# Attention before a routed expert layer: stacking queries and keys with their hash bits into one 71-row contraction, and using the exp tile as the stationary operand for V

## The chip, the cores and the metric

The kernel runs on one core of a Trainium2 chip. The metric is the device time of one execution in microseconds (us). A unit in this text is one pass of the attention's main loop.

## The reference

Attention over four batches of eight heads (768 positions, 64 dimensions). Each query and key gets six hash bits (the signs of a projection), and a query sees only the keys with the same six bits. A query that no key matches gets the mean of V; for its sake both kernels add a tiny multiple of the sums of V. The result feeds a layer of eight experts whose weights come from a Sinkhorn iteration.

```python
q_bits = (np.einsum('bhsd,dk->bhsk', q, proj) > 0)
k_bits = (np.einsum('bhsd,dk->bhsk', k, proj) > 0)
mask   = q_bucket[:, :, :, None] == k_bucket[:, :, None, :]
scores = np.where(mask, scale * (q @ k.T), -1e9)
attn   = softmax(scores) @ v
x      = attn.transpose(0, 2, 1, 3).reshape(B * S, H * D)     # 3072 x 512
P      = sinkhorn(exp(x @ w_gate))                            # 8 rounds
out    = sum(P[:, e:e+1] * (relu(x @ w1[e]) @ w2[e]) for e in range(8))
```

Both kernels write the mask as arithmetic. Bits are coded as plus or minus one half and one side is scaled by a large constant, so that the product of the bits, with a constant row beside them, is zero when all six agree and far below zero when one differs. It is added to the score by the same accumulation on TensorE, and exp then gives zero.

## The kernel before

Work goes by groups: one batch and half of its heads (four), eight groups in all. A unit is a group, a chunk of 256 queries and two key tiles, so there are 72 units. While batches 1, 2 and 3 are in attention, the first expert's matmuls of the batch before are put between the units; the text calls these pieces filler (16 pieces of four 128x384 matmuls, 12 of four 128x512, per batch). The experts' own part follows the attention and takes two thirds of the time.

```python
def scores(n, qc, kp, pairs):              # one unit: both score buffers, two exps
    for hs in pairs:
        st = [sps.tile([P, 2, 2 * QC], F32, tag="s", name="st") for _ in range(len(hs) // 2)]
        for kk in range(2):
            for part in range(3):          # hash bits, then two halves of 32 dimensions
                for i, h in enumerate(hs):
                    lw = d["kb"][sl, ks] if part == 0 else d["k"][sl, part - 1, ks]
                    rw = d["qb"][sl, qs] if part == 0 else d["q"][sl, part - 1, qs]
                    pin(nc.tensor.matmul(st[i // 2][:, i % 2, kk * QC:(kk + 1) * QC], lw, rw,
                                         start=(part == 0), stop=(part == 2), skip_group_check=True))
        for s_ in st:
            pt = wk.tile([P, 2, 2 * QC], F16, tag="p", name="pt", bufs=4)
            pin(nc.scalar.activation(out=pt, in_=s_, func=Act.Exp, scale=scale))
# ... (cut) values(): V slices of 32 columns are stationary and the exp tile moves;
#     a third pass with a tile of ones gives the denominator, which two transposes
#     and a reciprocal on VectorE turn into a factor for the normalising step
for u, (n, qc, kp) in enumerate(units):    # main loop, cut
    nxt = scores(*units[u + 1], four if b else two) if u + 1 < len(units) else None
    values(n, qc, kp, pts)
    pts = nxt
    for _ in range(2):
        next(prep, None)                   # a step of the next group's preparation
    if left > 0:
        got, end = take(fill, left / slots - 200)   # filler
```

The preparation of the next group transposes k and q in blocks of 32x32 on VectorE (L209, 0.95 us for each 128x768), casts them on GpSimd and computes the bits. Four heads lie side by side in four strips of 32 rows, which is how the matmuls read them: no copy is needed.

The softmax here doesn't subtract the row's maximum and nothing guards it: scores larger than these inputs give would overflow.

Of the kernel before, what the change touches and what calls it, by code (L numbers as in the profile page):

```python
# [19 lines left out]
def kernel(  # L20
# [35 lines left out]
    QC = 256  # L56
    NQC = S // QC
    KP = KT // 2
# [9 lines left out]
    pb = consts.tile([P, 2, P], F32)  # L68
# [5 lines left out]
    for a in range(HG):  # L74
        sl = slice(32 * a, 32 * (a + 1))
        for o in (0, 8):
            nc.vector.tensor_copy(pb[sl, :, 32 * a + o:32 * a + o + NB], proj4[sl])
# [4 lines left out]
    nc.vector.tensor_scalar(row_i, row_i, 31, None, op0=Alu.bitwise_and)  # L82
    row_f = consts.tile([P, 1], F32)
    nc.vector.tensor_copy(row_f, row_i)
    coef = consts.tile([P, 1], F32)
    thr = consts.tile([P, 1], F32)
    step = consts.tile([P, 4], F32)
    for i, edge in enumerate((NB - 0.5, NB + 0.5, 7.5, 7.5 + NB)):
        nc.vector.tensor_scalar(step[:, i:i + 1], row_f, edge, None, op0=Alu.is_lt)
    nc.vector.tensor_scalar(thr, step[:, 0:1], 1.0, 1e30, op0=Alu.subtract, op1=Alu.mult)  # L90
    nc.vector.tensor_scalar(coef, step[:, 0:1], 2.0 * BIG - 2.0 * NB * (BIG / 2.0), None, op0=Alu.mult)
    for i, w in ((1, 2.0 * NB * (BIG / 2.0)), (2, BIG), (3, -BIG)):
        nc.vector.scalar_tensor_tensor(coef, step[:, i:i + 1], w, coef, op0=Alu.mult, op1=Alu.add)
    ones = consts.tile([P, P], F32)
    nc.gpsimd.memset(ones, 1.0)
    ones16 = consts.tile([P, R], F16)
    nc.gpsimd.memset(ones16, 1.0)
# [10 lines left out]
    def load_w(e, which, pin=False):  # L108
        if which == 1:
            t = wpool.tile([P, DO, F], F16, tag="w1")  # L110
            src = moe_w1[e].rearrange("(g h c d) f -> g c h d f", g=NGRP, h=HG, c=2)
            for do in range(DO):
                ins = nc.gpsimd.dma_start(out=t[:, do, :], in_=src[do // 2, do % 2])  # L113
                if pin:
                    tc.keep_in_program_order(ins)
            pin = False
        else:
            t = wpool.tile([P, FO, DD], F16, tag="w2")
            ins = nc.gpsimd.dma_start(out=t, in_=moe_w2[e].rearrange("(fo fi) d -> fi fo d", fi=P))
        if pin:  # L120
            tc.keep_in_program_order(ins)
        weights[e, which] = t
# [45 lines left out]
    ld = actx.enter_context(tc.tile_pool(name="ld", bufs=3))  # L168
    lv = actx.enter_context(tc.tile_pool(name="lv", bufs=2))
    wk = actx.enter_context(tc.tile_pool(name="wk", bufs=2))  # L170
    sps = actx.enter_context(tc.tile_pool(name="sps", bufs=2, space=PSUM))
    avs = actx.enter_context(tc.tile_pool(name="avs", bufs=1, space=PSUM))
# [19 lines left out]
    def prepare(n):  # L192

        d = grp[n] = {}
        v16 = wk.tile([P, HG, KT, D], F16, tag="v16")
        vs32 = wk.tile([P, HG, 3, D], F32, tag="vs32", bufs=1)
        vs16 = wk.tile([P, HG, D], F16, tag="vs16")
        for name in ("k", "q"):
            tr = wk.tile([P, 2, S], F32, tag="tr")
            src = nat[name, n]  # L200
            for c in range(2):
                i_ap = src[:, :, 32 * c:32 * (c + 1)]
                o_ap = tr[:, c, :]
                if name == "k":
                    i_ap = i_ap.rearrange("p (m t) d -> p m t d", m=M4)
                    o_ap = o_ap.rearrange("p (t m r) -> p m t r", t=KT, m=M4)
                else:
                    o_ap = o_ap.rearrange("p (m r) -> p m r", r=R)
                pin(nc.vector.transpose(o_ap, i_ap))  # L209
                yield None  # L210
            t16 = wk.tile([P, 2, S], F16, tag=name + "16", name=name + "16")
            for c in range(2):
                nc.gpsimd.tensor_copy(t16[:, c, :], tr[:, c, :])
            bt = wk.tile([P, S], F16, tag=name + "b", name=name + "b")
            for i in range(2):
                sl = slice(i * HT, (i + 1) * HT)
                pr = ops.tile([P, 512], F32, tag="o", name="pr")
                for c in range(2):
                    pin(nc.tensor.matmul(pr[:, 0:HT], pb[:, c, :], tr[:, c, sl], start=(c == 0), stop=(c == 1)))  # L219
                if name == "k":  # L220
                    pin(nc.vector.tensor_scalar(bt[:, sl], pr[:, 0:HT], thr[:, 0:1], coef[:, 0:1],
                                                op0=Alu.is_gt, op1=Alu.mult))
                else:
                    pin(nc.vector.tensor_scalar(bt[:, sl], pr[:, 0:HT], 0.0, 0.5,
                                                op0=Alu.is_gt, op1=Alu.subtract))
                yield 640
            d[name], d[name + "b"] = t16, bt
        for i in range(2):
            nc.gpsimd.tensor_copy(v16[:, 2 * i:2 * i + 2].rearrange("p h t d -> p h (t d)"), nat["v", n, i])
        nc.gpsimd.tensor_tensor(vs32, v16[:, :, 0:3, :], v16[:, :, 3:6, :], op=Alu.add)  # L230
        nc.gpsimd.tensor_tensor(vs32[:, :, 0], vs32[:, :, 0], vs32[:, :, 1], op=Alu.add)
        nc.gpsimd.tensor_tensor(vs16, vs32[:, :, 0], vs32[:, :, 2], op=Alu.add)
        yield None
        vp = ops.tile([P, 512], F32, tag="o", name="vp")
        for c in range(2):
            for h in range(HG):
                pin(nc.tensor.matmul(vp[32 * h:32 * (h + 1), c:c + 1], vs16[:, h, 32 * c:32 * (c + 1)],
                                     ones16[:, 0:1], start=True, stop=True))
        vs = wk.tile([P, 2], F32, tag="vs")
        pin(nc.vector.tensor_scalar(vs, vp[:, 0:2], EPS, None, op0=Alu.mult))  # L240
        d["v"], d["vs"] = v16, vs
        yield 300

    def scores(n, qc, kp, pairs):
        d = grp[n]
        tiles = []
        for hs in pairs:
            st = [sps.tile([P, 2, 2 * QC], F32, tag="s", name="st") for _ in range(len(hs) // 2)]
            for kk in range(2):
                for part in range(3):  # L250
                    for i, h in enumerate(hs):
                        sl = slice(32 * h, 32 * (h + 1))
                        qs = slice(qc * QC, (qc + 1) * QC)
                        ks = slice((2 * kp + kk) * P, (2 * kp + kk + 1) * P)
                        lw = d["kb"][sl, ks] if part == 0 else d["k"][sl, part - 1, ks]
                        rw = d["qb"][sl, qs] if part == 0 else d["q"][sl, part - 1, qs]
                        pin(nc.tensor.matmul(st[i // 2][:, i % 2, kk * QC:(kk + 1) * QC], lw, rw,  # L257
                                             start=(part == 0), stop=(part == 2), skip_group_check=True))
            for s_ in st:
                pt = wk.tile([P, 2, 2 * QC], F16, tag="p", name="pt", bufs=4)  # L260
                pin(nc.scalar.activation(out=pt, in_=s_, func=Act.Exp, scale=scale))  # L261
                tiles.append(pt)
        return tiles

    av = {}

    def values(n, qc, kp, pts):
        d = grp[n]
        if kp == 0:
            av["n"] = avs.tile([P, 2, QC], F32, tag="n", name="num")  # L270
            av["d"] = avs.tile([P, QC], F32, tag="d", name="den")
        num, den = av["n"], av["d"]
        for kk in range(2):
            kt = 2 * kp + kk
            first, last = kt == 0, kt == KT - 1
            for part in range(3):
                for h in range(HG):
                    sl = slice(32 * h, 32 * (h + 1))
                    mv = pts[h // 2][:, h % 2, kk * QC:(kk + 1) * QC]
                    if part < 2:  # L280
                        pin(nc.tensor.matmul(num[sl, part, :], d["v"][:, h, kt, 32 * part:32 * (part + 1)], mv,  # L281
                                             start=first and part == 0, stop=last, skip_group_check=True))
                    else:
                        pin(nc.tensor.matmul(den[sl, :], ones16, mv, start=first, stop=last))  # L284
        if kp == KP - 1:
            b, g = groups[n]
            dt = wk.tile([P, QC], F32, tag="dt")
            pin(nc.vector.transpose(dt, den))
            r8 = wk.tile([P, QC // R], F32, tag="r8")
            pin(nc.vector.tensor_scalar(r8, dt.rearrange("p (a r) -> p a r", r=R)[:, :, 0], S * EPS, None,  # L290
                                        op0=Alu.add))
# [272 lines left out]
```

## Time and profile before

| | before |
|---|---|
| time, median (lowest to highest) | 901.59 us (900.67 to 903.22), 4 runs |
| span of the profiled run | 899.6 us |
| first exp of the attention starts | 27.6 us |
| last exp ends | 284.7 us |
| last gate to the end (experts) | 610.9 us |

The first lines are from the page: busy time of each engine, then the chain of waits that ended last as shares of the span, then groups of instructions by line (busy time, mean of one in ns, then the idle time before them and what ended it).

```profile
PE 830.8 (92%) x7120; PEld 443.1 (49%) x7120; DVE 475.7 (53%) x886; ACT 383.4 (43%) x643; POOL 154.1 (17%) x151
...
PE 63%; DVE 8%; issue 1%; ACT 0%
...
L261 ACT ACTIVATE pt<-st 128x1024 f16<-128x1024 f32 x144 | 139.5, 1021 | 141.4 <-PE st L257 141.1
...
L219 PE MATMUL pr<-tr,pb 128*128 128x384 f32 x128 | 49.8, 528 | 14.9 <-DVE tr L209 9.4
```

ScalarE (ACT) spends 139.5 us in exp and stands idle as long again, 141.4 us, before exps, nearly all of it for the scores (25.6 us of it before the first one). Of the 257 us from the first exp to the last the exps have 54%. The chain of waits could be followed back only to 238 us here, so it says nothing of the first three batches. L219 is the fp32 product that gives the hash bits.

The next view gives busy time by engine in three stretches: the attention of batch 1, the experts from the last gate on, and a piece from the middle of the experts.

```profile
core 0: us, PE busy (x) PEld busy (x) DVE busy (x) ACT busy (x) POOL busy (x), PEclk, DMA share, GB/s
91.00:156.00 65.00, 61.58 (x982) 34.46 (x978) 34.16 (x71) 32.94 (x34) 15.25 (x20) 1.00 0.37 88
288.70:899.60 610.90, 580.02 (x3031) 297.12 (x3028) 329.83 (x572) 241.06 (x494) 80.25 (x58) 0.98 0.18 32
340.00:600.00 260.00, 258.19 (x1361) 132.80 (x1359) 140.03 (x235) 114.34 (x231) 36.04 (x27) 1.00 0.19 28
```

In the middle of the experts TensorE (PE) is busy 258 of 260 us: there is little to win there without taking matmuls away, and the change takes none. In the attention exp is busy 33 of 65 us. The timeline, with the first exp of all and then one unit of batch 1, shows why both cannot be full:

```profile
27.62 1.94 ACT L261 ACTIVATE pt<-st 128x1024 f16<-128x1024 f32 x2 [25.60 <-PE st L257]
...
165.12 0.29 PE L257 MATMUL st<-qb,kb 32*128 32x256 f16 x4
...
166.05 1.94 ACT L261 ACTIVATE pt<-st 128x1024 f16<-128x1024 f32 x2 [3.95 <-PE st L257]
...
168.07 0.29 PE L257 MATMUL st<-qb,kb 32*128 32x256 f16 x4
...
169.00 1.02 ACT L261 ACTIVATE pt<-st 128x1024 f16<-128x1024 f32 x1 [1.00 <-PE st L257]
```

The scores start at 165.12, the two exps run from 166.05 to 167.99, and the next scores start at 168.07. One unit fills both score buffers, so scores and exp take turns: 2.95 us per unit, of which exp is 1.94.

### The profile page before, as it was taken

Reading aid. Unit: us, or ns where it says so; the run is one execution under the profiler, and the core shown is the slowest. Engines: PE = TensorE matmul, PEld = TensorE weight load, DVE = VectorE, ACT = ScalarE, POOL = GpSimd, SP = SyncE. Lnnn points to the kernel's source line nnn. Section 1 sums busy time; section 2 is a strip of 40 time slices with the busy share of each in tenths; the row PEclk is TensorE's granted clock in tenths of the full one; section 3 lists DMA queues with packets and bytes.
Section 4 is the critical chain, followed back from the end, with each engine's and each line's share of the span. In section 5 each row is a group of like instructions: output and inputs, shape, how many; then the busy total and the mean of one; then the engine's idle time right before and its main releaser. Section 6 shows DMA issues by size and latency. Waiting matters only on the chain.

```text
span 899.6 us, 16739 instructions
## 1 busy us (share of the span) xinstructions
PE 830.8 (92%) x7120; PEld 443.1 (49%) x7120; DVE 475.7 (53%) x886; ACT 383.4 (43%) x643; POOL 154.1 (17%) x151
## 2 busy tenths in 40 slices
PE   3788999999899879999999999999999999999992
PEld 1455554555555435555555555555555555555541
DVE  3334564554755765555555555555555555555551
ACT  0466455455465435554333343333333333333330
POOL 3442131221201340014004001400310140000000
PEclk9799999999999889999999999999999999999997
DMA  6941343620000213033003302400330140001222
GB/s 176 190 132 63 102 84 73 152 70 5 1 3 2 33 16 47 1 43 52 1 1 48 47 1 30 65 1 1 48 48 1 20 75 2 1 1 46 78 81 78
DMA packets 37362, 43.07 MB, mean 48 GB/s; under 512 B 15784, under 2 KB 28072, under 8 KB 37288
## 3 DMA queue, kind: packets, MB, share of 16 engines
q0 software_dynamic: 27328, 16.84, 13.1%
q1 hardware_dynamic: 9960, 25.17, 9.3%
q8 instruction: 55, 0.90, 0.4%
q14 instruction: 19, 0.16, 0.1%
HBM read 52.45 MB, written 6.29 MB: 65 GB/s over the span
## 4 chain that ended last, share of the span: by engine, by line
PE 63%; DVE 8%; issue 1%; ACT 0%
PE yp L140 31%; PE a L474 15%; PE d L474 12%; DVE hT L483 3%; PE st L257 1%; PE num L281 1%; PE yp L328 1%; DVE p L413 1%; PE hp L320 1%; PE hp L161 0%; DVE rs L410 0%; DVE xT L298 0%; DVE p L423 0%; DVE xd L440 0%; PE cpt L418 0%
## 5 line engine op out<-in xcount | busy, mean ns | idle before, releaser
L140 PE MATMUL yp<-t,hT 128*128 128x512 f16 x1392 | 375.1, 380 | 0.0
L479 ACT COPY u<-a 128x384 f32<-128x384 f32 x336 | 161.1, 480 | 255.9 <-PE a L474 251.3
L483 DVE CUSTOM_DVE_ANT_0 hT<-d,u 128x384 f16<-128x384 f32 x336 | 179.3, 554 | 144.7 <-PE d L474 88.4
L261 ACT ACTIVATE pt<-st 128x1024 f16<-128x1024 f32 x144 | 139.5, 1021 | 141.4 <-PE st L257 141.1
L140 PEld LDWEIGHTS <-hT 128*128 128x128 f16 x1392 | 136.4, 98 | 116.7 <-issue 0.9
L146 DVE SCALAR_TENSOR_TENSOR acc<-yp,p,acc 128x512 f32<-128x512 f32 x168 | 125.9, 749 | 114.6 <-PE yp L140 112.2
L474 PEld LDWEIGHTS <-t 128*128 128x128 f16 x896 | 87.8, 98 | 78.6 <-issue 11.2
L474 PE MATMUL d<-xd,t 128*128 128x384 f16 x448 | 109.3, 326 | 3.9
L474 PE MATMUL a<-xT,s 128*128 128x384 f16 x448 | 109.5, 326 | 0.0
L474 PEld LDWEIGHTS <-s 128*128 128x128 f16 x672 | 65.9, 98 | 83.4 <-issue 8.1
L509 ACT ACTIVATE hT<-a 128x384 f16<-128x384 f32 x112 | 55.0, 491 | 74.1 <-PE a L474 73.5
L113 POOL DMA_DIRECT2D t<-in_moe_w_dram x32 | 21.4, 675 | 297.1 <-PE d L474 287.8
L257 PE MATMUL st<-q,k 32*128 32x256 f16 x1152 | 63.6, 274 | 0.0
L219 PE MATMUL pr<-tr,pb 128*128 128x384 f32 x128 | 49.8, 528 | 14.9 <-DVE tr L209 9.4
L281 PE MATMUL num<-pt,v 128*32 128x256 f16 x1152 | 53.3, 277 | 9.5 <-DVE xT L298 9.2
L257 PE MATMUL st<-qb,kb 32*128 32x256 f16 x576 | 55.1, 277 | 3.7 <-ACT pt L261 1.7
L474 PE MATMUL d<-xT,t 128*128 128x384 f16 x224 | 55.1, 328 | 0.0
L474 PE MATMUL a<-xT,t 128*128 128x384 f16 x224 | 55.1, 328 | 0.0
L474 PE MATMUL a<-xd,s 128*128 128x384 f16 x224 | 54.8, 326 | 0.0
L284 PE MATMUL den<-pt,ones 128*32 128x256 f16 x576 | 41.1, 275 | 0.0
L219 PEld LDWEIGHTS pr<-tr,pb 128*128 128x128 f32 x128 | 23.4, 197 | 35.5 <-DVE tr L209 15.0
L257 PEld LDWEIGHTS <-k 32*128 32x128 f16 x1152 | 38.9, 95 | 1.9
(73 smaller groups left out, 545.5 us busy)
## 6 DMA issues: line engine op xcount, KB each, us to landing
t<-in_moe_w_dram POOLq DMA_DIRECT2D x8, 1024.0 KB, 9.1
t<-in_moe_w_dram POOLq DMA_DIRECT2D x32, 256.0 KB, 10.4
k<-in_k_dram SPq DMA_DIRECT2D x8, 768.0 KB
q<-in_q_dram SPq DMA_DIRECT2D x8, 768.0 KB
v<-in_v_dram SPq DMA_DIRECT2D x32, 192.0 KB
out_dram<-acc SPq DMA_DIRECT2D x24, 256.0 KB
wg_sb<-in_moe_w_gate_dram POOLq DMA_DIRECT2D x4, 2.0 KB, 8.8
proj<-in_proj_dram SPq DMA_DIRECT2D x2, 3.0 KB
```

The source lines that it names most:

```text
L113: ins = nc.gpsimd.dma_start(out=t[:, do, :], in_=src[do // 2, do % 2])
L140: yield nc.tensor.matmul(yp, hT[:, fo, j * P:(j + 1) * P], w2[:, fo, :], start=(fo == 0), stop=(fo == FO - 1))
L146: nc.vector.scalar_tensor_tensor(out=acc[:, blk, :], in0=yp, scalar=pw[:, blk, e:e + 1], in1=acc[:, blk, :], op0=Alu.mult, op1=Alu.add)
L219: pin(nc.tensor.matmul(pr[:, 0:HT], pb[:, c, :], tr[:, c, sl], start=(c == 0), stop=(c == 1)))
L257: pin(nc.tensor.matmul(st[i // 2][:, i % 2, kk * QC:(kk + 1) * QC], lw, rw, start=(part == 0), stop=(part == 2), skip_group_check=True))
L261: pin(nc.scalar.activation(out=pt, in_=s_, func=Act.Exp, scale=scale))
L281: pin(nc.tensor.matmul(num[sl, part, :], d["v"][:, h, kt, 32 * part:32 * (part + 1)], mv, start=first and part == 0, stop=last, skip_group ...
L284: pin(nc.tensor.matmul(den[sl, :], ones16, mv, start=first, stop=last))
L474: yield nc.tensor.matmul(bk, wq[wn][:, do, f * P:(f + 1) * P], xq[xn][:, do, :], start=first and do == 0, stop=do == 1, skip_group_check=True)
L479: nc.scalar.copy(t, bk)
L483: add(TENSOR_ADD_SAT, out=dst, in0=bk, in1=u, s0=3e38, s1=0.0)
L509: nc.scalar.activation(out=hT[:, f, hi], in_=a, func=Act.Relu)
```

## The change

The intent is to break that chain. A score tile becomes one contraction of 71 rows (64 dimensions, six bits, one constant row), so a unit is one head and one key tile with one score buffer, and the next unit's scores run while exp works. There are 192 units. The exp tile becomes the stationary operand and V, with a column of ones, moves in 65 columns: the denominator comes out in the last column, already one per query, and needs no transposes. The price is that each score matmul reads the 71 rows of a head as one block, so they have to be put under each other. Copies by DMA (called stacking copies below) bring the strips of 32 rows into that place, and the bits go through a scratch tensor in DRAM.

```diff
-            for i in range(2):
-                pr = ops.tile([P, 512], F32, tag="o", name="pr")
-                for c in range(2):
-                    pin(nc.tensor.matmul(pr[:, 0:HT], pb[:, c, :], tr[:, c, sl], start=(c == 0), stop=(c == 1)))
+                nc.gpsimd.tensor_copy(t16[:, c, :], tr[:, c, :])
+                for h in range(HG):
+                    nc.sync.dma_start(out=st[32 * c:32 * (c + 1), h, :], in_=t16[32 * h:32 * (h + 1), c, :])
+                yield None
+            for c in range(2):
+                for j in range(HG):
+                    pin(nc.tensor.matmul(pr[32 * j:32 * (j + 1), 0:QT], pb[:, c].rearrange("p a r -> p (a r)"),
+                                         tr[:, c, j * QT:(j + 1) * QT], start=(c == 0), stop=(c == 1)))
+            if name == "k":
+                pin(nc.vector.tensor_scalar(bt, pr[:, 0:QT], 0.0, 0.5, op0=Alu.is_gt, op1=Alu.subtract))
+                nc.gpsimd.tensor_scalar(bt, bt, BIG, None, op0=Alu.mult)
+            ds = scr.tile([HG, HG, 8, QT], F16, tag="ds", name="ds")
+            nc.sync.dma_start(out=ds.rearrange("j h r t -> (j h r) t"), in_=bt)
+            for h in range(HG):
+                nc.sync.dma_start(out=st[D:KR, h, :].rearrange("r (j t) -> r j t", j=HG),
+                                  in_=ds[:, h, 0:NB + 1, :].rearrange("j r t -> r j t"))
 ... (cut: V goes to `va` with its column of ones, its sums to `vs`, on GpSimd)
-    def scores(n, qc, kp, pairs):      ... 24 matmuls of 32 rows, two exps 128x1024
+    def scores(n, h, kt):
+        st = sps.tile([P, 2, 512], F32, tag="s", name="st")
+        for i in range(2):
+            pin(nc.tensor.matmul(st[:, i, 0:HT], d["k"][0:KR, h, kt * P:(kt + 1) * P],
+                                 d["q"][0:KR, h, i * HT:(i + 1) * HT], start=True, stop=True))
+        pin(nc.scalar.activation(out=pt, in_=st[:, :, 0:HT], func=Act.Exp, scale=scale))
-    def values(n, qc, kp, pts):        ... V and ones stationary, exp tiles moving
+    def values(n, h, kt, pt):
+        for j in range(J):
+            pin(nc.tensor.matmul(num[:, j * (D + 1):(j + 1) * (D + 1)], pf[:, j * P:(j + 1) * P],
+                                 va[:, h, kt, :], start=False, stop=(kt == KT - 1), skip_group_check=True))
 ... (cut: reciprocal and multiply per head; turn(), six 128x128 transposes per two heads)
+            if i == 20:
+                drain(prep)
+                if n + 2 < len(groups):
+                    fetch(n + 2)
+        if i % 2 == 1 and i > 1:
+            next(prep, None)
```

Per group this adds 26 DMAs on SyncE's (SP) queue: for k and again for q eight stacking copies of 32x768, one write of the bits, four reads of the bits.

## The prediction

> **What bounds it now.** The expert part (288 us to the end, 611 us) is PE back to back (windows: busy 258 of 260 us from 340 to 600); the change leaves it alone. The change acts on attention. First exp starts at 27.6 us; the batches' gates start at 89.5, 157.9, about 222 and 288 us (timeline): 63 us for the batch without filler matmuls, 65 to 67 for the three with. ACT is busy only 33 of 65 us[...]. The timeline shows a serial chain: a unit's scores take both score buffers, so scores (0.77, plus 0.2 until exp), two exps (1.94), then the next scores: 165.12 to 168.06 = 2.94 us. 18 units are 53 us; the fp32 hash products add four blocks of 2.6 us per batch between units.
>
> **What the change does.**
> - Scores: two 384-column matmuls per unit (192 units of one head and key tile). 128x384 matmuls pace at 0.161 us here (filler), so 0.32 us per unit.
> - Values: six 128-column weight loads with 65-column matmuls. The gate's 24 load/matmul pairs start 25 ns apart; I estimate 30 ns, 0.18 us per unit.[...]
> - Exp: 1.021 us less 256 x 0.83 ns (slope of the 384 and 512 column copies): 0.81 us, pitch 0.76; 192 are 146 us against 140 now. But scores of the next unit now overlap exp.
> - The denominator, its transposes and the value-sum matmuls go. A start matmul per head (0.17), transposes (1.5 us per batch) and their copies come.
> - Hash products: 2.6 us falls to 0.7 to 2.6.
> - Stacking costs 26 DMAs per group on SP (issue 0.33 to 0.48 us each here), with a bounce through DRAM. [...]here the projection load took 2.0 us from end of issue to use.
>
> **Sum (estimates).** Unit without filler: exp end, values, scores, exp start: 0.82 us, exp-bound. With a filler piece: PE-bound, 0.32+0.18+0.65 or 0.87: 1.17 or 1.39. Per filled batch: 16x1.17 + 12x1.39 + gate 1.3 + 15x0.82 + four transposing units 3.5 = 52.5; hash, starts and waits bring 57 to 60. Batch without filler: 40 plus waits for stacked operands. These are the risk: in the scheduled order the k bits wait on POOL behind the value sums, then DRAM write, a 768 KB prefetch ahead in the queue, and the read: about 20 us from transposes to usable operands, the length of an unfilled group (24 x 0.82). I allow 2 to 5 us of stall per group end in batch 0, first exp near 31 us. Attention ends near 255 instead of 288.
>
> **Predicted: 866 us, 80% range 846 to 886.** Faster over 2%: 0.86; within: 0.13; slower: 0.01.
>
> **What shows it.** 192 exps of 0.81 us; ACT idle in batch 0 only at group ends, before scores waiting for bit DMAs; values pairs near 30 ns; filled batches 57 to 60 us, PE-bound; 611 us from last gate to end; first exp 29 to 35 us.
>
> **What would make it wrong.** Weight loads not hidden behind 65-column matmuls[...]; DMA chains longer than a group everywhere; filler held by DVE (0.95 us transposes before evacuations); weight loads shifting in the expert part.

The gate's pairs, from which the 30 ns come, have 8 columns (128x8 in the trace before), not 65. On PE's 61 of 65 us the trace before shows that the record of a filler matmul of 128x384 lasts 0.33 us (L320, mean 327 ns) while they start 0.16 us apart (four of them take 0.81 us), so the busy time counts more than the spacing needs.

## The result

| | before | after |
|---|---|---|
| time, median (lowest to highest) | 901.59 us (900.67 to 903.22), 4 runs | 886.83 us (885.83 to 889.05), 4 runs |
| ratio | | 0.9838, 95% interval 0.9813 to 0.9862 |
| span of the profiled run | 899.6 us | 887.3 us |
| first exp starts | 27.6 us | 39.9 us |
| gates of the four batches | 90.3, 158.7, 227.1, 288.7 | 104.3, 164.7, 224.8, 276.5 |
| last exp ends | 284.7 us | 273.0 us |
| last gate to the end | 610.9 us | 610.8 us |

Ratios are the mean time of one kernel's fast runs over that of the other's fast runs of the same rounds, so they are not quite the ratio of the medians. The change gained 1.6%, which is 15 us (12 us between the two profiled runs, which the times below come from); the prediction said 36 us and its range ended at 886. The first batch ends 14 us later than before, and the three others get back 26.

The same lines of the page, for the kernel after, with the line that says which engines the chain of waits runs through:

```profile
PE 794.9 (90%) x5392; PEld 431.9 (49%) x5392; DVE 440.8 (50%) x787; ACT 392.4 (44%) x691; POOL 143.0 (16%) x138
...
PE 73%; DMA 9%; DVE 7%; SPq 4%; POOL 2%; ACT 2%; issue 1%; POOLq 0%; ACTq 0%; DVEq 0%
...
L248 ACT ACTIVATE pt<-st 128x768 f16<-128x768 f32 x192 | 149.1, 809 | 120.8 <-PE st L245 120.3
...
L245 PE MATMUL st<-qs,ks 71*128 71x384 f16 x384 | 102.1, 350 | 52.6 <-DMA qs<-ds 46.4
```

Exp still waits 120.8 us before its 192 tiles, 37.8 of it before the first one. PE now waits 46.4 us for `qs<-ds`, the reads that bring the q bits out of DRAM. In the chain DMAs have 9% of the span (4% are the loads of V) and SP's sequencer 4%. This can't be set against the line of the kernel before, whose chain was followed only over the last 73% of its span.

The windows of the kernel after, for the experts and for three stretches of batch 0:

```profile
62.70:69.50 6.80, 0.95 (x8) 0.62 (x9) 0.00 (x0) 0.03 (x1) 0.00 (x0) 0.68 0.48 158
69.50:75.00 5.50, 5.50 (x46) 3.62 (x44) 2.06 (x4) 4.02 (x5) 1.65 (x2) 0.50 0.29 106
75.00:90.70 15.70, 14.22 (x192) 9.55 (x190) 6.46 (x13) 13.97 (x19) 6.77 (x8) 0.99 0.35 107
276.50:887.30 610.80, 581.00 (x3034) 297.45 (x3032) 334.52 (x584) 241.40 (x495) 68.84 (x40) 0.98 0.16 32
```

The last row answers the row of the experts before: 610.8 against 610.9 us. From 62.7 to 69.5 no engine computes (there are eight matmuls). After this PE runs at half its clock (0.50) for 5.5 us, and only then does exp fill its engine, 13.97 of 15.70 us. The timeline of ACT across the two group ends of batch 0 shows it unit by unit, after the first exp of all:

```profile
39.90 1.51 ACT L248 ACTIVATE pt<-st 128x768 f16<-128x768 f32 x2 [37.83 <-PE st L245]
...
56.08 6.58 ACT L248 ACTIVATE pt<-st 128x768 f16<-128x768 f32 x9 [0.76 <-PE st L245]
69.47 0.81 ACT L248 ACTIVATE pt<-st 128x768 f16<-128x768 f32 x1 [6.80 <-PE st L245]
70.44 0.81 ACT L248 ACTIVATE pt<-st 128x768 f16<-128x768 f32 x1 [0.16 <-PE st L245]
...
84.15 6.58 ACT L248 ACTIVATE pt<-st 128x768 f16<-128x768 f32 x9 [0.76 <-PE st L245]
97.88 0.81 ACT L248 ACTIVATE pt<-st 128x768 f16<-128x768 f32 x1 [7.14 <-PE st L245]
```

Nine exps take 6.58 us, so exps follow each other every 0.72 us without a gap (the 6.58 end where the last one ends, 0.81 after its start; neighbours overlap a little). This is what the change wanted. At the group ends stand waits of 6.80 and 7.14 us, and behind them a pitch of 0.97 us with PE at half clock (granted 0.50, from 65.1 to 75.4 us and again from 92.4 to 102.7). Two further group ends, in batches 1 and 2, cost 3.6 and 3.8 us of exp idle.

What SP did before the wait of 7.14 us, in the order of its queue:

```profile
73.30 8.07 SPq L212 DMA_DIRECT2D ks<-t  x8
82.78 0.35 SPq L226 DMA_DIRECT2D ds<-kb  x1
83.24 0.37 SPq L182 DMA_DIRECT2D k<-in_k_dram  x1
84.32 1.31 SPq L228 DMA_DIRECT2D ks<-ds  x4
85.73 5.57 SPq L212 DMA_DIRECT2D qs<-t  x8
91.40 0.54 SPq L226 DMA_DIRECT2D ds<-qb  x1
91.98 0.43 SPq L182 DMA_DIRECT2D q<-in_q_dram  x1
93.16 1.31 SPq L228 DMA_DIRECT2D qs<-ds  x4
```

SP starts at 73.30 and is done at 94.47 us. The copies of q begin only after k's bits were written, landed and were read back; q's bits are written at 91.40 although VectorE had them at 84.1; and the last reads wait for that write to land. The k transposes had started at 71.41 and the scores of group 2 could start at 96.96: 25.5 us from transposes to operands. Of these, 1.9 pass before SP's first copy; SP issues for 14.8 (two loads for a later group among them) and waits for 6.4, of which 4.6 are for GpSimd; and the last reads take 2.5 to land. The work that should hide this chain ended at 90.73 us, 19.3 us after the transposes. The difference, plus 0.9 us from the scores' start to exp's, is the wait: 25.5 - 19.3 + 0.9 = 7.1 us.

The issue times by themselves are in the view of the tile that the k copies write (least, median and greatest time in ns, then first and last start):

```profile
L212 SPq DMA_DIRECT2D ks<-t x64: 507/588/5115, 10.4 to 229.1; - x64
L228 SPq DMA_DIRECT2D ks<-ds x32: 272/299/1219, 27.3 to 234.1; - x32
```

A copy of 32x768 takes SP 0.59 us to issue, not the 0.33 to 0.48 us that the prediction took from the loads of k and q (768 KB each). The kernel before held a nearer example: its loads of V (192 KB each) took 0.56 us, the median of 32. Nor is the time fixed: one copy took 5.1 us, at 10.4 us, where the first loads of V and of the weights were under way. One more thing stands in the way, on GpSimd, in the timeline of the group before:

```profile
49.76 0.83 POOL L233 CAST va<-v 128x768 f16<-128x768 f32 x1 [3.37 <-DMA v<-in_v_dram]
50.67 1.47 POOL L236 TENSOR_TENSOR v<-va 128x768 f32<-128x768 f16 x1
...
53.83 0.68 POOL L222 TENSOR_SCALAR kb<-kb 128x192 f16<-128x192 f16 x1
54.58 1.59 POOL L210 CAST t<-tr 128x768 f16<-128x768 f32 x2
```

The scaling of the k bits (53.83), whose input was ready at 50.2, and the casts of q (54.58) stand behind the cast of V, which waited for its load, and behind the sums of V.

So the candidates for the missing 20 us are: the serial issue of the stacking copies on SP; the bounce of the bits through DRAM; the order on GpSimd; and, at the start, the traffic of the first expert's weights, whose second load the scheduler moved up to 2.74 us because nothing holds it back.

### The profile page after: what moved, and what is told of

The parts are those of the page before. It is cut to its first block, busy times and chain, and to the rows that moved or that the text cites. A ratio compares the mean times of both kernels' runs of the same rounds, so it can differ in the third digit from the quotient of the medians.

```text
span 887.3 us, 13608 instructions
## 1 busy us (share of the span) xinstructions
PE 794.9 (90%) x5392; PEld 431.9 (49%) x5392; DVE 440.8 (50%) x787; ACT 392.4 (44%) x691; POOL 143.0 (16%) x138
## 4 chain that ended last, share of the span: by engine, by line
PE 73%; DMA 9%; DVE 7%; SPq 4%; POOL 2%; ACT 2%; issue 1%; POOLq 0%; ACTq 0%; DVEq 0%
PE yp L139 31%; PE a L462 16%; PE d L462 13%; PE st L245 4%; DMA v<-in_v_dram 4%; DVE hT L471 4%; PE yp L309 3%; SPq L212 2%; DMA qs<-ds 2%; PE num L264 2%; DMA ds<-qb 2%; ACT pt L248 2%; PE hp L301 2%; DMA ds<-kb 1%; PE hp L160 1%
## 5 line engine op out<-in xcount | busy, mean ns | idle before, releaser
L139 PE MATMUL yp<-t,hT 128*128 128x512 f16 x1392 | 375.1, 380 | 0.0
L248 ACT ACTIVATE pt<-st 128x768 f16<-128x768 f32 x192 | 149.1, 809 | 120.8 <-PE st L245 120.3
L245 PE MATMUL st<-qs,ks 71*128 71x384 f16 x384 | 102.1, 350 | 52.6 <-DMA qs<-ds 46.4
L497 ACT ACTIVATE hT<-a 128x384 f16<-128x384 f32 x112 | 54.9, 490 | 75.4 <-PE a L462 74.8
L264 PEld LDWEIGHTS <-pt 128*128 128x128 f16 x1152 | 65.1, 102 | 30.4 <-issue 7.8
L245 PEld LDWEIGHTS <-ks 71*128 71x128 f16 x384 | 34.9, 102 | 75.5 <-issue 40.3
L264 PE MATMUL num<-va,pt 128*128 128x65 f16 x1152 | 70.5, 200 | 0.0
L118 POOL DMA_DIRECT2D t<-in_moe_w_dram x16 | 13.7, 859 | 334.4 <-PE d L462 291.0
L301 PE MATMUL hp<-xT,t 128*128 128x384 f16 x192 | 39.1, 326 | 0.0
L309 PE MATMUL yp<-t,hT 128*128 128x512 f16 x144 | 39.1, 396 | 0.0
L304 DVE TENSOR_SCALAR hT<-hp 128x384 f16<-128x384 f32 x48 | 26.4, 551 | 19.6 <-PE hp L301 19.6
## 6 DMA issues: line engine op xcount, KB each, us to landing
ks<-ds SPq DMA_DIRECT2D x32, 10.5 KB
```

The source lines that it names most:

```text
L139: yield nc.tensor.matmul(yp, hT[:, fo, j * P:(j + 1) * P], w2[:, fo, :], start=(fo == 0), stop=(fo == FO - 1))
L245: pin(nc.tensor.matmul(st[:, i, 0:HT], d["k"][0:KR, h, kt * P:(kt + 1) * P], d["q"][0:KR, h, i * HT:(i + 1) * HT], start=True, stop=True))
L248: pin(nc.scalar.activation(out=pt, in_=st[:, :, 0:HT], func=Act.Exp, scale=scale))
L264: pin(nc.tensor.matmul(num[:, j * (D + 1):(j + 1) * (D + 1)], pf[:, j * P:(j + 1) * P], va[:, h, kt, :], start=False, stop=(kt == KT - 1), ...
L301: pin(nc.tensor.matmul(hp[:, 0:HT], w1[:, do, fo * P:(fo + 1) * P], xT[:, do, b * S + t * HT:b * S + (t + 1) * HT], start=(do == 0), stop= ...
L304: pin(nc.vector.tensor_scalar(hT[:, fo, t * HT:(t + 1) * HT], hp[:, 0:HT], 0.0, None, op0=Alu.max))
```

## The experiments

Each kernel below is the changed kernel plus the edit shown; those from `c2` on build on `c1_all_pinned`. First exps and waits are from the timeline of ACT. Where a text names a theory by a letter, the sentence ahead of it says which cause is meant. The kernels without a note gave a correct result.

### Weights at the start, and the order on GpSimd

The first edit tests the theory that the early weight load delays the start: pinning the gate's load keeps the weight load behind it.

```diff
-    nc.gpsimd.dma_start(out=wg_sb, in_=...)
+    pin(nc.gpsimd.dma_start(out=wg_sb, in_=...))
```

> Changed kernel with one pin on the gate-weight load, so that the first expert's 1 MB w2 load no longer floats to 2.7 us on the POOL queue but comes after the first group's preparation; by the built order this also puts the second group's key fetch behind the first group's stacking DMAs. Theory A (late start comes from that load and that fetch filling the DMA engines while the stacking DMAs wait): first exp moves from 39.9 to 28 to 33 us, total 887 falls to 877 to 881, the stalls at the group ends (6.8 and 7.1 us of exp idle in batch 0) stay. Rival B (late start comes from the query casts waiting on POOL behind the V data): V lands earlier too, so the start moves only 2 to 4 us. Rival C (the serial SP issues): start moves under 2 us.

Measured: 894.31 us, ratio to before 0.9927 (0.9889 to 0.9965). The first exp starts at 38.0 us instead of 39.9, and a new wait of 12.7 us appears at 153.8 us: the scheduler, given one more fixed instruction, also put the next group's k load later and the casts of V earlier. The waits of batch 0 became 9.1 and 6.5 us. The start moved by 1.9 us, less than this theory needed; the total says little, because the edit moved other things.

The second edit tests the theory that the order on GpSimd lengthens the chain. It fixes the program's order for the casts of k, q and V and for the scaling of the k bits, so that V comes last.

```diff
-                nc.gpsimd.tensor_copy(t16[:, c, :], tr[:, c, :])
+                pin(nc.gpsimd.tensor_copy(t16[:, c, :], tr[:, c, :]))
-                nc.gpsimd.tensor_scalar(bt, bt, BIG, None, op0=Alu.mult)
+                pin(nc.gpsimd.tensor_scalar(bt, bt, BIG, None, op0=Alu.mult))
-            nc.gpsimd.tensor_copy(va[...], nat["v", n, i]...)
+            pin(nc.gpsimd.tensor_copy(va[...], nat["v", n, i]...))
```

> Changed kernel with POOL's work of one preparation pinned in the order k casts, k bit scaling, q casts, V casts and sums. Theory A (group-end stalls come from k scaling and q casts standing on POOL behind V casts that wait for V, and behind the V sums): exp idle at the ends of groups 0 and 1 falls from 6.8 and 7.1 us to under 2 each, those later (3.6, 3.8) to under 1, total falls by 15 to 20 us to 867 to 872. Rival B (26 SP issues of 0.6 us in series per group): stalls stay above 5 us, total 882 to 888. Rival C (DRAM bounce latency): likewise stay above 4 us.

Measured: 881.97 us, ratio 0.98 (0.9761 to 0.984), 4.9 us below the changed kernel's median of another call (the intervals of the ratios overlap). The two waits of batch 0 fell from 6.8 and 7.1 us to 3.3 and 2.8 us, not to under 2 as the theory had it; a wait of 2.0 us came up inside the second group; the first exp did not come earlier (41.0 us). The order on GpSimd is shown to be a part of the waits at the group ends, and by itself none of the late start.

Both edits together:

> Both pins. If both theories A hold, the gains add: first exp 26 to 32 us, no stall over 2 us, total 857 to 864. If SP issue is the next limit (its 32 issues of one group are about 16 us against 17.8 us for an unfilled group), stalls of 2 to 5 us stay in batch 0 and the total is 864 to 870.

Measured: 877.96 us, ratio 0.9747 (0.9716 to 0.9777); first exp 35.7 us; waits of 5.3, 3.2, 2.4 and 4.6 us. Alone, the edits moved the start by 1.9 us forward and 1.1 us back; together they brought it 4.2 us forward, so each alone left something else in the way.

The fourth edit takes the bounce away by reading the bits from a constant tile. The result is wrong.

```diff
-            nc.sync.dma_start(out=ds..., in_=bt)
-            ... four reads st <- ds
+            ... four reads st <- ident (a constant tile, 42 pieces of 256 bytes each)
```

> Wrong result on purpose: changed kernel with the bit rows filled from a constant tile, so no DRAM write, no wait on it and no wait on the hash products; everything else stacked as before, V work still ahead on POOL. Theory A (POOL order, with the bounce a smaller part): stalls in batch 0 shrink by about 3 us each to 3 to 4 us, total 872 to 880. Rival C (the bounce is the main part): stalls go to under 1 us, total 862 to 868. Rival B (SP issues): one issue fewer per name, so under 2 us per stall, total 880 to 885.

Measured: 890.76 us, ratio 0.989 (0.9853 to 0.9928), waits of 2.1, 6.5, 8.7, 5.4 and 5.8 us. With fewer dependencies the scheduler ordered the rest anew, so the run answers nothing. For this reason the next kernels fix the whole order.

### A basis in fixed order, and one dose more of serial issue

`c1_all_pinned` is `a3_both` with every DMA on SP pinned in program order.

> The both-pins kernel with every DMA of fetch and preparation pinned in program order on SP, as a base that the next two change by one thing each without the scheduler moving others. The reads of the k bits now wait for their DRAM write ahead of the q stacking (2.3 us more in the chain). Exp idle at group ends 4 to 8 us in batch 0, total 876 to 886.

Measured: 879.06 us, ratio 0.976 (0.9714 to 0.9807); first exp 36.2 us; waits of 3.8, 4.1, 5.2 and 2.0 us. It is as fast as `a3_both` within the intervals, and now one thing can be changed at a time. The 2.3 us of this text and the next is an estimate: in the changed kernel 1.5 to 2.8 us passed from the start of a write of bits to the first read behind it in five of the first six cases (5.6 in the other), with other issues of SP between them; in `c1` it was 1.7 for the k bits (17.08 to 18.80 and 76.39 to 78.11), 1.2 of them from the end of the write's issue.

`c2_pinned_no_bounce` is the fourth edit on this basis. Its output is wrong, which doesn't matter for the time.

> Wrong result on purpose: the all-pinned kernel with the bit rows read from a constant tile, so two DRAM writes of 0.5 us issue and two waits of 2.3 us drop out of the SP chain of each group (about 5.5 us). Theory (the chain on SP, issue and bounce waits added, must fit in a group): stalls of batch 0 shrink by 5 us each to 0 to 2, total 860 to 870. Rival (issues alone): shrink by under 2 us, total within 5 us of the all-pinned kernel.

Measured: 874.21 us, ratio 0.9709 (0.9677 to 0.974), first exp 32.7 us. But the four substitute reads, in pieces of 256 bytes, took 3.4 us of issue instead of 1.3, so the edit added serial issue while it took the bounce away. Inconclusive; `e1` below mends it.

`c3_pinned_doubled` issues every stacking copy of k twice, the second time into rows that nobody reads, and changes nothing else.

```diff
+                    if name == "k":
+                        pin(nc.sync.dma_start(out=st[72 + 24 * c:96 + 24 * c, h, :],
+                                              in_=t16[32 * h:32 * h + 24, c, :]))
```

> The all-pinned kernel with each k stacking DMA issued a second time (24 of its 32 rows) into rows of the stacked tile that nobody reads: 8 more issues of about 0.59 us, 4.7 us per group. Theory (SP's serial issues are in the chain): start 4.7 us later, each stalled group end 4 to 5 us longer, total 15 to 28 us above the all-pinned kernel. Rival (only latencies count, issues overlap them): under 4 us in all.

Measured: 919.81 us, ratio 1.0208 (1.0168 to 1.0247), 41 us more than `c1` in the same rounds, where the text had 15 to 28. The first exp starts at 41.4 us, 5.2 later; the waits of batch 0 grew to 10.7 and 10.6 us, and those of the filled batches to 4.1, 7.0, 5.0, 4.5 and 3.1 us. SP's queue before group 2:

```profile
79.31 0.59 SPq L212 DMA_DIRECT2D ks<-t  x1
79.94 0.82 SPq L214 DMA_DIRECT2D ks<-t  x1
80.81 0.56 SPq L212 DMA_DIRECT2D ks<-t  x1
81.41 0.75 SPq L214 DMA_DIRECT2D ks<-t  x1
...
98.74 4.96 SPq L212 DMA_DIRECT2D qs<-t  x8
103.81 0.54 SPq L228 DMA_DIRECT2D ds<-qb  x1
```

The extra copies (L214) take 0.75 to 0.82 us each and stand between the real ones. Eight of them are some 6 us per group, and the chain of group 2, from k transposes to scores, became 29.8 us instead of 23.3. Six us in each of eight groups are 48; 41 arrived in the time. SP's issue is in line with the scores: this is the strongest single result. It isn't quite issue alone, since the extra copies also move data: SP's issues of the chain grew by 5.3 us (13.1 to 18.3), and the wait for the write of the k bits by 1.5 (1.2 to 2.7).

### Fewer issues

`c4_dram_stack` stacks the rows through DRAM too: two writes of 128x768, two reads that bring all four heads, and the bits as before. That is 18 DMAs per group instead of 26. The order changes with it: the rows of q are now written before the rows and the bits of k are read, so that the bounce of the k bits has something beside it. It also starts each preparation earlier and moves the first expert's weights to the second group.

```diff
-                for h in range(HG):
-                    nc.sync.dma_start(out=st[32 * c:32 * (c + 1), h, :], in_=t16[32 * h:32 * (h + 1), c, :])
+                pin(nc.sync.dma_start(out=rows[c].rearrange("h r s -> (h r) s"), in_=t16[:, c, :]))
+            for c in range(2):
+                pin(nc.sync.dma_start(out=st[32 * c:32 * (c + 1)], in_=rows[c].rearrange("h r s -> r h s")))
 ... (cut: the steps now run k rows, k bits, q rows, reads of k, q bits, reads of q)
-            if i == 20:
+            if i == 14:
                 drain(prep)
-        if i % 2 == 1 and i > 1:
+        if i > 1:
             next(prep, None)
+                if n == 1:
+                    load_w(0, 1, pin=True)      # from before the loop
```

> An attempt at a better kernel on the all-pinned base: operands are stacked through DRAM with 2 writes and 2 reads per tensor instead of 8 copies (18 DMAs per group instead of 26, 7.6 us of issue instead of 15), the preparation is pulled every unit from the third on and the next fetch issued at unit 14 instead of 20, and the first expert's weight loads wait until the second group. First exp at 19 to 24 us, no exp idle over 2 us at group ends, batch 0 in 36 to 38 us, later batches 53 to 56, total 832 to 845. If the DRAM route is slower than I think (reads of 32 rows over 4 us), stalls of 2 to 4 us remain in batch 0 and the total is 845 to 855.

Measured: 857.34 us, ratio 0.9518 (0.9495 to 0.954). The first exp starts at 24.3 us, earlier than before the change. One wait of 7.0 us is left, at 69.1 us, where the weight loads run. The time is above both ranges of the text (832 to 845, 845 to 855): a miss.

The three parts of it, each alone on `c1`:

> The all-pinned kernel with only the stacking route changed: 18 DMAs per group instead of 26, same start of the preparation, same weight loads. If the count of SP issues is what makes the chain long, 8 issues less at 0.59 and less queueing take 4 to 6 us off the chain: stalls of batch 0 under 1 us, first exp 27 to 33 us instead of 36, total 860 to 870.

> The all-pinned kernel with only the earlier preparation and fetch (steps every unit from the third, fetch at unit 14), its 26 DMAs per group and the early weight loads kept. If the stalls at group ends come from the length of the operand chain, starting it earlier by about 6 units takes 3 to 5 us off each: stalls 0 to 2, first exp unchanged near 36, total 864 to 872. If SP's total issue time per group (about 16 us plus waits) is the limit whatever the start, 874 to 882.

> The all-pinned kernel with only the first expert's loads moved from the start to the second group. If their traffic holds back the DRAM bounce of the first bits (5.5 us from issue of the write to the read in the all-pinned kernel against 1.7 later), first exp moves from 36.2 to 31 to 33 us; a stall of about 7 us may come back in the second group. Total 875 to 884.

| part alone on `c1` (879.06 us) | time | ratio to before | first exp (`c1`: 36.2) | main waits at group ends |
|---|---|---|---|---|
| stacking through DRAM (`d3`) | 866.83 us | 0.9628 (0.9601 to 0.9655) | 27.6 | 4.6, 2.9 (and 5.4 before a gate) |
| earlier preparation (`d2`) | 876.58 us | 0.9735 (0.9716 to 0.9755) | 36.7 | 3.8, 6.3 |
| first weights later (`d4`) | 875.60 us | 0.9724 (0.9708 to 0.9741) | 29.6 | 12.2 in batch 0 |

The route with fewer issues is worth 12 us by itself and brings the first exp 8.6 us forward; what of this is the number of issues and what the new order of the steps was not told apart. The earlier preparation measured 2.5 us less and later weights 3.5 us less, neither shown to differ from `c1` (the intervals overlap). `d2` hardly does what it was meant to do: the k transposes of group 2 start 3.0 us after the first exp of their group, against 3.2 in `c1`, because they wait for the load of k, which stands behind the last reads in SP's queue. So an earlier start of the chain was not tested. Later weights bring the first exp 6.5 us forward, so they do delay the start once the order is fixed, but they then meet the preparation of group 2 and a wait of 12.2 us gives nearly all of it back. Together the three gave 21.7 us, a little more than their sum of 18.

`d1_staged_weights` is `c4` with the two weight loads one group apart, after each preparation.

> The DRAM-stack kernel with only the place of the first expert's loads changed: w1 issued at unit 16 of group 0, w2 at unit 16 of group 1, instead of both at the start of group 1, where their 4 MB of reads delayed the row writes (6.6 us of SP issue for two) and left 7 us of idle exp before group 2. Expected: that stall under 2 us, batch 0 near 50 us from 24.3, total 845 to 851. Rival (the 7 us come from something else in that group): total within 3 us of the DRAM-stack kernel's 857.

Measured: 856.01 us, ratio 0.951 (0.9482 to 0.9539), with waits of 3.5 and 4.7 us where under 2 us were expected. The wait of 7.0 us was split in two, not removed, and the time is that of `c4`, as the rival in the text had it. A miss.

### The bounce, the weights and V

`e1_no_bounce_same_reads` is `c1` with the bits read from a DRAM tile that is filled once: the same four reads of the same shape, but no write before them, and no wait for the write or for the hash products. Wrong on purpose.

```diff
-            ds = scr.tile([HG, HG, 8, QT], F16, tag="ds", name="ds")
-            pin(nc.sync.dma_start(out=ds.rearrange("j h r t -> (j h r) t"), in_=bt))
+            ds = fixed
```

> Wrong result on purpose: the all-pinned kernel with the bit rows read by the same four DMAs (7 rows of four 384-byte pieces) from a DRAM tile filled once at the start, so that per group two DRAM writes, their issue (0.5 us each) and their waits (1.2 us or more each) go and nothing else. If the bounce is an in-line part of the chain of 3 to 5 us, stalls of batch 0 go from 3.8 and 4.1 to 0 to 1.5 us, first exp from 36.2 to 28 to 32, total 862 to 870. If only the issues count: stalls change by about 1 us, total 874 to 880.

Measured: 865.51 us, ratio 0.9586 (0.9553 to 0.9619), against 879.06 us and 0.976 for `c1`. It was run at another time. The first exp starts at 31.6 us, 4.5 earlier; the waits of batch 0 are 4.8 and 2.1 us, and those of the filled batches are gone. SP before group 2:

```profile
63.85 8.75 SPq L215 DMA_DIRECT2D ks<-t  x8
72.65 1.52 SPq L230 DMA_DIRECT2D ks<-fixed  x4
74.27 6.40 SPq L215 DMA_DIRECT2D qs<-t  x8
80.72 1.52 SPq L230 DMA_DIRECT2D qs<-fixed  x4
```

No pause stands between the copies and the reads any more. The chain is 20.4 us (61.96 to 82.41) instead of 23.3 in `c1`. The write, its landing, the wait for the bits and the order that they force on SP's queue cost about 14 us in all (16 by the ratios).

`e2_spread_weights` is `d1` with the first weight matrix in two halves, one in each of the first two groups, and the second one at the start of the third.

```diff
... (cut: the tile for both halves, and the gate's weights)
+            if i == 16 and n < 2:
+                pin(nc.gpsimd.dma_start(out=weights[0, 1][:, 2 * n:2 * n + 2], in_=w1v[:, 2 * n:2 * n + 2]))
-            if i == 16 and n == 1:
+            if i == 0 and n == 2:
                 load_w(0, 2, pin=True)
```

> The staged-weights kernel with w1 of the first expert loaded in two halves (unit 16 of groups 0 and 1) and w2 at the start of group 2. If DMA traffic makes the 3.5 and 4.7 us of idle exp in its batch 0, they fall to under 2 each, total 848 to 853; w2 may arrive late for the filler of batch 1 (needed about 25 us after its load), which would show as PE waiting in front of the yp matmuls. If traffic is not the cause, total within 2 us of 856.

Measured: 854.95 us, ratio 0.948 (0.9446 to 0.9514), a little above what was expected and within 2 us of 856, where the text had put it if traffic is not the cause; waits of 2.0, 2.0 and 3.8 us; first exp 24.3 us. Its SP queue before group 2, then what stands before the gate of batch 0, then its exps:

```profile
52.39 1.19 SPq L214 DMA_DIRECT2D rows<-t  x2
57.93 0.32 SPq L231 DMA_DIRECT2D ds<-kb  x1
60.29 1.18 SPq L214 DMA_DIRECT2D rows<-t  x2
61.58 0.88 SPq L238 DMA_DIRECT2D ks<-rows  x2
62.55 1.31 SPq L240 DMA_DIRECT2D ks<-ds  x4
```

```profile
76.10 1.84 DVE L212 STREAM_TRANSPOSE tr<-k 128x768 f32<-128x768 f32 x2 [3.58 <-DMA k<-in_k_dram]
...
78.43 0.72 PE L309 MATMUL lg<-wg_sb,xT 128*128 128x8 f16 x21 [3.70 <-DVE xT L302]
```

```profile
L270 ACT ACTIVATE pt<-st 128x768 f16<-128x768 f32 x192 | 148.9, 809 | 83.2 <-PE st L267 80.8
```

Two writes (1.2 us of issue together) and two reads (0.9 us) do what eight copies of 0.59 us each, 4.7 us, did (all 18 issues of the group take 7.9 us, where the text of `c4` had 7.6), and while the k bits land, SP issues the rows of q. The 192 exps are as they were in the changed kernel (809 ns) but wait 83.2 us instead of 120.8. The operands of group 2 come in time here. The wait of 3.8 us is another: VectorE waits 3.58 us for the k load of a later group, with the copy of `xT` behind it in its queue, which the gate needs. That load was issued at 67.85 us, behind two weight loads (65.78 and 66.58), and landed 8.2 us later. The 5.4 us in `d3` are of the same kind. This is the fastest kernel, correct, 5.2% faster than before by its ratio. It is not shown to differ from `d1` and `c4`, whose intervals overlap with it.

`e3_v_after_rows` fetches the V of the first group after the rows were written.

> The same with V of the first group fetched after the row writes of the first stacking instead of before. If the first reads wait because the row writes queue behind V (issued 11.6, read at 17.0), first exp moves from 24.2 to 19 to 21 us; V's casts and sums then end near 23 us and hold the first values matmuls, so the total falls by 1 to 4 us against the spread-weights kernel.

Measured: 861.39 us, ratio 0.9555 (0.9535 to 0.9574). The first exp came later, at 29.8 us. In its trace the loads of V are issued at 12.6 to 15.1 us, right before the reads, and the reads of the k bits take 4.64 us to issue instead of 1.31; that this is the cause was not tested. A miss: the order of `e2` was the better one.

### The chain and the wait, side by side

All from batch 0: when group 2's k transposes start, counted from the first exp of group 1; the chain from there to group 2's first scores; how long the exps of group 1 take; and the exp idle at the end of group 1.

| kernel | SP issues per group | transposes start | chain | exps of group 1 | exp idle |
|---|---|---|---|---|---|
| `c3`, copies of k doubled | 34 | 3.1 us | 29.8 us | 23.2 us | 10.6 us |
| changed kernel | 26 | 2.0 us | 25.5 us | 21.3 us | 7.1 us |
| `a2`, GpSimd order | 26 | 2.0 us | 23.8 us | 23.6 us | 2.8 us |
| `d2`, earlier preparation | 26 | 3.0 us | 23.8 us | 21.4 us | 6.3 us |
| `c1`, all in fixed order | 26 | 3.2 us | 23.3 us | 23.2 us | 4.1 us |
| `d4`, weights later | 26 | 2.9 us | 22.3 us | 23.6 us | 2.2 us |
| `c4`, three changes at once | 18 | 4.8 us | 22.6 us | 21.3 us | 7.0 us |
| `c2`, bits from a constant tile | 24 | 4.7 us | 22.2 us | 21.3 us | 6.6 us |
| `a3`, both first edits | 26 | 2.0 us | 21.6 us | 21.3 us | 3.2 us |
| `d3`, stacking through DRAM | 18 | 2.7 us | 20.5 us | 21.2 us | 2.9 us |
| `e1`, no bounce | 24 | 3.4 us | 20.4 us | 22.7 us | 2.1 us |
| `e2`, weights spread | 18 | 2.3 us | 19.1 us | 22.7 us | none |

The chain alone does not give the wait. The second and third columns together, less the fourth, and 0.6 to 0.9 us from the scores' start to exp's, do. Where the transposes start late (`c4`, `c2`), they wait for the load of k (2.8 and 2.7 us). In `a2`, `c1`, `c3` and `d4` the group takes about 2 us more because a wait of that length stands inside it, so a part of what they save at the group end is lost before it.

## Why the prediction was wrong

**What was right.** The experts' part stayed at 611 us. The 192 exps take 0.81 us each. The pairs of weight load and 65-column matmul start 29 ns apart (six take 0.345 us, one 0.200, so (0.345 - 0.200)/5), against an estimate of 30, while the record of one load lasts 102 ns (L264, mean), so the loads did hide. Six transposes of 128 columns take 0.50 us and one 0.219, so their pairs start 56 ns apart (L279). Scores and exp overlap: 0.72 us per unit in batch 0 where nothing waits, better than the 0.82 that was said. A hash product takes 0.86 us in 13 of 16 cases, all at a granted clock of 1.00 (mean of its window); the first two take 1.73 and the third 1.51, all within the 0.7 to 2.6. Around the third, at 48.3 us, six values matmuls take 0.54 us, as they do at a clock of 0.50 after the wait (0.34 to 0.35 at 1.00), though the trace has 1.00 there too. Batch 3 took 51.7 us from gate to gate, where the sum without waits had given 52.5; batches 1 and 2, which contain a long group end each, took 60.4 and 60.1 us, just over the 57 to 60 of the text. The two long waits of batch 0 stand at the ends of groups and end with the reads of the bits, as the text had said; a wait of 2.0 us inside the first group (at 50.7 us, behind a hash product) it had not. One reading of the kernel before was off: the third gate starts at 226.3 us, not at about 222.

**The step that failed.** It is the term for the operand chain: "about 20 us from transposes to usable operands, the length of an unfilled group (24 x 0.82). I allow 2 to 5 us of stall per group end in batch 0, first exp near 31 us." The mechanism was named and its size was too small:

- The chain is 25.5 us, not 20. The text costed an issue on SP at 0.33 to 0.48 us, read from the loads of k and q, so 26 of them at 8.6 to 12.5; SP issues for 14.8 us within the chain. The stacking copies take 0.59 us, and sixteen of them, ten other issues, two landings and 4.6 us of waiting for GpSimd stand in one queue. `c3` shows that SP's issue is in line (41 us for eight more issues per group), `d3` that the route through DRAM, with its order, saves 12 us, `e1` that the bounce costs about 14 us, and `a2` that the order on GpSimd was over half of the two waits at the group ends of batch 0. These do not add: each shortens the same chain, and by the arithmetic of the wait nothing more is to be had once the chain fits in a group.
- The wait at each group end of batch 0 is 6.8 and 7.1 us: 13.9 us where about 7 were in the sum. The arithmetic of the wait is the one shown above: with a chain of 20 us it would have been 1.6 us (20 - 19.3 + 0.9).
- The first exp starts at 39.9, not 31 us. With `c1` fixed in order, the route (`d3`, 8.6 us), the weights (`d4`, 6.5 us) and the bounce (`e1`, 4.5 us) each move it. They lie along one chain, so these need not add either.
- After the waits of 7 us PE ran at half clock. PE stood idle for 6.61 us until 68.55; the granted clock went to 0.50 at 65.1 us and came back to 1.00 at 75.4. At the next group end PE stood for 6.95 us until 96.96, and the clock was 0.50 from 92.4 to 102.7 us. Behind both waits exps have a pitch of 0.97 instead of 0.72 us. What sets these times was not tested. The prediction did not have this term: the exps of the first two groups took 44.0 us without the wait of 6.8 between them, where 39.4 (48 x 0.82) had been said. The units at a pitch of 0.97 us, at the start and after the wait, the wait of 2.0 us and some single waits outweigh those at 0.72.

The sum closes: the first exp of group 2 was said for 31 + 39.4 + 7 = 78 us and came at 97.9. Of these 20 us the start is 9, the two waits are 7 and the slower units are 4.6. From there to the last exp it took 175 us, and 177 had been predicted (255 - 78). The miss lies in batch 0, the only one without filler to hide the chain; the text's own warning, "DMA chains longer than a group everywhere", came true there.

**What stays open.** How the waits of batch 0 divide between DMA traffic and the number of issues was not told apart: issues and landings were both longer where other loads were under way (the copy of 5.1 us; the landings in `c1`, 1.2 us when quiet and 5.0 us with the weight loads, from end of issue to the read), and `a4` and `c2` gave no answer. What is left in `e2` is at least in part no longer the operand chain but a late load of k, by its trace; no run changed that load alone.

## What to carry to other kernels

When a change turns an arrangement in place into copies, cost the copies by the time that their queue needs to issue them one after the other, with every wait that the queue must sit through, and set that sum against the length of the work that should hide it. Measure one issue of the very shape, because here a copy of 48 KB took 0.59 us to issue, more than most loads of 768 KB did (0.33 to 0.56), a read of the bits (10.5 KB) 0.30, and the small ones are many. And look first at the stage that has nothing else to do: a chain that filler mostly hides in three batches stood open in the fourth.
